# First MLP's weights, split a whole slice at a time, with one buffer place per slice

## The chip, the cores and the metric

The kernel runs on one core of one Trainium2 chip. The metric is the device time of one launch in microseconds (us); lower is better. Three runs of the kernel before took 896.28, 899.64 and 904.32 us, and their median, 899.64 us, is the time before.

## The reference

Windowed attention (4 batches, 8 heads, 576 positions, head dimension 64; the first four heads see the last 32 positions, the last four every fourth of the last 128), then two MLPs, 512 to 2048 to 512, over all 2304 tokens, in float32:

```python
attn = softmax(where(masks, q @ k.T / sqrt(64), -1e9))
x = concat_heads(attn @ v)                 # 2304 x 512
h = maximum(x @ w_in, 0.0)
x = (h * h) @ w_out                        # first MLP
h = x @ w_in2
out = (h * cos(h)) @ w_out2                # second MLP
```

## The kernel before

Attention is cut into 48 units (4 batches, 4 head pairs, 3 groups of 192 queries). A unit goes through eight steps (`unit`, L184): S matmuls (L198, and for the first twelve units a mask matmul, L205), row maximum on VectorE (DVE, L219, L221), three Exp on ScalarE (ACT, L225), reciprocal and product on DVE (L230 to L237), a transpose on TensorE (PE, L242), a copy on ACT (L245), the value matmuls (L254), and the split of the result into two float32r parts, `xh` by a cast on ACT (L281) and `xl` by a subtraction on DVE (L283).

The 2304 tokens are five blocks of 512, 384, 512, 512 and 384 columns (`SIZES`), the hidden layer 16 slices of 128 (`fc`). One step of a block is one slice: `product1` (L305) makes a slice of h with 12 matmuls (4 chunks of 128 rows, times wh·xh, wh·xl, wl·xh), `middle` (L317) applies the activation and splits the result into `gh` (ACT, L351) and `gl` (DVE, L353), `product2` (L359) adds the slice to y with 12 more. The first twelve units are all of the first block's tokens, so its `product1` has to wait for them; the other 36 are worked in between the steps of the first four blocks.

Weights come as 64-bit words. `load_w` (L99) loads one half of a slice (i = 0 is w_in, i = 1 is w_out; 512 KB) with one DMA on SyncE's queue (SP). `split_w` (L108) turns it into the parts wh and wl in four steps: two DVE instructions that build a float32 (L116, L119), a third (L122), a cast on ACT (L125) and a subtraction on DVE (L127), each on 512 columns. The words lie in a pool of three buffers (`raw`, shared with `store` and `load_x`), but the first six halves (`RAW_EARLY`) and the first twelve units (`N_EARLY`) lie in places of weights of later slices (`early`, L91). The parts of one half have one tile, `w{fc}_{i}`; the second MLP's weights go into the same tiles when the last block of the first MLP is through with them.

The order of the work is written by hand. `at` puts a call on a list with a time in steps (16 steps to a block; t = 0 is the first block's start), and `in_steps` does so for a generator's parts. `before` turns a number on a finer scale into a time before t = 0. The list is sorted and run. Up to t = 0 and from t = 96 each engine's instructions stand in just that order; between these, for the first MLP and the first block of the second, the framework's scheduler may move an instruction ahead of one that its own model holds up (L505 to L509). Every engine and the SP queue work in order. The weights' times are:

```python
EARLY_LOADS = (2.5, 3.5, 6.62, 8.91, 10.16, 11.56)
EARLY_SPLITS = (5.5, 7, 17.91, 21.32, 23.16, 24.98)
t = h / 2 - 1.573                        # later halves, h = 2 * fc + i
times = [t + d for d in SPLIT]           # SPLIT = (0, 0.05, 0.2, 0.62)
at(split_at[h - 3] + 0.01 ..., load_w, *w)
```

An entry of `EARLY_LOADS` is a place among the units' loads, which are numbered 1 to 11: 3.5 is between units 3 and 4.

Of the kernel before, what the change touches and what calls it, by code (L numbers as in the profile page):

```python
# [7 lines left out]
F32 = mybir.dt.float32  # L8
F32R = mybir.dt.float32r
BF16 = mybir.dt.bfloat16  # L10
U32 = mybir.dt.uint32
# [5 lines left out]
P = 128  # L17
B, H, S, D = 4, 8, 576, 64
DM, DFF = 512, 2048
# [4 lines left out]
KT = 96  # L24
# [3 lines left out]
UQ = TPU * QT  # L28
UK = QT * (TPU - 1) + KT
UP = TPU * 2 * QT  # L30
UV = TPU * 2 * D
# [5 lines left out]
NF = DFF // P  # L37
# [3 lines left out]
SLOT = [0, 2, 1, 0, 2]  # L41
PACE = [n / max(SIZES) for n in SIZES]
N_EARLY = 12
RAW_EARLY = 6
SQUARE_ON_ACT = (0, 4)
LAG = (2, 3)
EPS = 1e-9
# [9 lines left out]
def attention_moe_moe(ctx: ExitStack, tc: tile.TileContext, units, masks, ident16_in, ident_in, w1, w2, out):  # L57
    nc = tc.nc
    pool = lambda name, bufs, **k: ctx.enter_context(tc.tile_pool(name=name, bufs=bufs, **k))
    const = pool("const", 1)  # L60
    wpool = pool("weights", 1)
    raw = pool("raw", 3)
    wtmp = pool("wtmp", 2)
# [16 lines left out]
    def at(t, f, *a):  # L80
        events.append((t, len(events), f, a))
# [6 lines left out]
    magic = const.tile([P, 1], F32, name="magic")  # L88
    y1 = [dram.tile([P, NC, n], F32, name=f"y1_{k}") for k, n in enumerate(SIZES)]

    def early(i):  # L91

        return dict(tag=f"w{NF - 1 - i // 2}_{1 - i % 2}", name="early")


    weights = {}
    raws = {}

    def load_w(m, fc, i):  # L99
        if m == 0 and 2 * fc + i < RAW_EARLY:  # L100
            t = wpool.tile([P, DM, 2], U32, **early(N_EARLY * 3 // 2 + 2 * fc + i))
        else:
            t = raw.tile([P, DM, 2], U32, tag="raw", name="wraw")
        raws[m, fc, i] = t
        nc.sync.dma_start(
            out=t, in_=(w1, w2)[m][fc, i].bitcast(U32).rearrange("p (n t) -> p n t", t=2))

    def split_w(m, fc, i):  # L108


        words = raws.pop((m, fc, i))
        low, high = words[:, :, 0], words[:, :, 1]
        parts = wpool.tile([P, 2, DM], F32R, tag=f"w{fc}_{i}", name=f"w{fc}_{i}")
        hi, lo = weights[m, fc, i] = parts[:, 0, :], parts[:, 1, :]
        t = wtmp.tile([P, DM], U32, tag="t", name="wt")
        nc.vector.tensor_scalar(  # L116
            out=t, in0=high, scalar1=3, scalar2=0x3FFFFFF8,
            op0=ALU.logical_shift_left, op1=ALU.bitwise_and)
        nc.vector.scalar_tensor_tensor(  # L119
            out=t, in0=high, scalar=0xC0000000, in1=t, op0=ALU.bitwise_and, op1=ALU.bitwise_or)  # L120
        yield
        nc.vector.scalar_tensor_tensor(  # L122
            out=t, in0=low, scalar=29, in1=t, op0=ALU.logical_shift_right, op1=ALU.bitwise_or)
        yield
        nc.scalar.copy(out=hi, in_=f32(t))  # L125
        yield
        nc.vector.tensor_tensor(out=lo, in0=f32(t), in1=f32(hi), op=ALU.subtract)  # L127
        yield


    xs = {}

    def block(m, k):
        if (m, k) not in xs:
            s = SLOT[k]
            xs[m, k] = tuple(
                ring.tile([P, NC, SIZES[k]], F32R, tag=f"x{n}{s}", name=f"x{n}{s}") for n in "hl"
            )
        return xs[m, k]
# [4 lines left out]
    def load_unit(u):  # L144
        if u >= N_EARLY:
            t = upool.tile([P, UQ + UK], F32, tag="uq", name="uq")
            nc.sync.dma_start(out=t, in_=units[u // UNITS, u % UNITS, :, :UQ + UK])
            loaded[u] = t, None
            return

        t = wpool.tile([P, UQ + UK], F32, **early(u // 2 * 3 + u % 2))
        nc.sync.dma_start(out=t, in_=units[0, u, :, :UQ + UK])
        if u == 0:
            nc.sync.dma_start(out=ident16, in_=ident16_in)
            nc.sync.dma_start(out=mask[:, :4 * KT], in_=masks[:, :4 * KT])
        loaded[u] = t
        if u % 2:
            v = wpool.tile([KT, 2, UV], F32, **early(u // 2 * 3 + 2))
            nc.sync.dma_start(
                out=v, in_=units[0, u - 1:u + 1, :KT, UQ + UK:].rearrange("u p n -> p u n"))  # L160
            for i in range(2):
                loaded[u - 1 + i] = loaded[u - 1 + i], v[:, i, :]
        if u == 1:
            nc.sync.dma_start(out=ident, in_=ident_in)
            nc.sync.dma_start(out=mask[:, 4 * KT:], in_=masks[:, 4 * KT:])
# [6 lines left out]
    def bank():  # L172
        return ps_h.tile([P, 512], F32, tag="h", name="h")

    def y_bank(e):
        return ps_y.tile([P, 512], F32, tag=f"y{e}", name=f"y{e}")
# [118 lines left out]
    def in_steps(times, key, steps, *a):  # L295
        for i, t in enumerate(times):
            at(t, *((resume, key) if i else (start, key, steps, *a)))
# [6 lines left out]

    def product1(m, k, fc):  # L305
        xh, xl = block(m, k)
        wh, wl = weights[m, fc, 0]
        h = hs[m, k, fc] = bank()[:, :SIZES[k]]
        for c in range(NC):
            for i, (w, x) in enumerate(((wh, xh), (wh, xl), (wl, xh))):  # L310
                nc.tensor.matmul(  # L311
                    h, w[:, c * P:(c + 1) * P], x[:, c, :],
                    start=c == 0 and i == 0, stop=c == NC - 1 and i == 2)
            if c:
                yield
# [42 lines left out]

    def product2(m, k, fc):  # L359
        gh, gl = gs.pop((m, k, fc))  # L360
        wh, wl = weights[m, fc, 1]
        if fc == 0:
            ys[m, k] = [y_bank(e)[:, :SIZES[k]] for e in range(NC)]
        y = ys[m, k]
        for e in range(NC):
            n = 0
            for w, g in ((wh, gh), (wh, gl), (wl, gh)):
                nc.tensor.matmul(  # L368
                    y[e], w[:, e * P:(e + 1) * P], g,
                    start=fc == 0 and n == 0, stop=fc == NF - 1 and n == 2,  # L370
                )
                n += 1
# [37 lines left out]
    before = lambda x: (x - 26.284) / 4.7  # L410

    load_unit(0)
    constants()
    for u in range(1, N_EARLY):
        at(before(-3.5 + 0.01 * u), load_unit, u)
# [14 lines left out]
    def later_by(t, d):  # L430

        while d:
            k = int(t // NF) if d > 0 else -int(-t // NF) - 1
            pace = PACE[k % NB]
            edge = (k + 1) * NF - t if d > 0 else k * NF - t
            move = d / pace
            if abs(move) <= abs(edge):
                return t + move
            t += edge
            d -= edge * pace  # L440
        return t
    for u in range(UNITS * B):
        if u < N_EARLY:
            t = 1.3 * u if u < 2 else 3.877 + 1.656 * (u - 2)
            times = [before(t + d) for d in (0, 1, 2.07, 2.87, 4.24, 4.95, 5.32, 6.2)]
        else:
            i = later.index(u)
            t, t1, t2 = place[i:i + 3]
            times = [t, *(later_by(t, d) for d in (0.25, 0.75, 0.8)),
                     t1 + 0.003, later_by(t1, 0.15), t2 - 0.003, later_by(t2, 0.42)]  # L450
            at(later_by(t, -1.5), load_unit, u)
            at(later_by(t, 0.6), load_values, u)
        in_steps(times, u, unit, u)


    EARLY_LOADS = (2.5, 3.5, 6.62, 8.91, 10.16, 11.56)
    EARLY_SPLITS = (5.5, 7, 17.91, 21.32, 23.16, 24.98)
    SPLIT = (0, 0.05, 0.2, 0.62)
    split_at = []
    for h in range(2 * NF):  # L460
        w = (0, h // 2, h % 2)
        if h < RAW_EARLY:
            at(before(-3.5 + 0.01 * EARLY_LOADS[h]), load_w, *w)
            times = [before(EARLY_SPLITS[h] + d) for d in (0, 0.6, 1.35, 2.24)]
        else:
            t = h / 2 - 1.573
            times = [t + d for d in SPLIT]
            at(split_at[h - 3] + 0.01 if h >= RAW_EARLY + 3 else before(-1. + 0.01 * h), load_w, *w)
        split_at.append(times[0])
        in_steps(times, ("w", *w), split_w, *w)  # L470
    t1 = NB * NF

    N_FAST = 12
    split_at = sorted(
        (t1 - NF + 1.2 + 1.3 * fc + 0.7 * max(fc - N_FAST, 0) + 1.8 * i, (1, fc, i))
        for fc in range(NF) for i in range(2)
    )
    for h, (t, w) in enumerate(split_at):
        in_steps([t + d for d in SPLIT], ("w", *w), split_w, *w)
        at(t - 1.5, load_w, *w)  # L480
    for m in range(2):
        for k in range(NB):
            t = (m * NB + k) * NF
            for fc in range(NF):
                times = [t + fc] * (NC - 1)
# [96 lines left out]
```

## Time and profile before

| | us |
|---|---|
| median of three runs | 899.64 |
| the profiled execution, whole | 898.14 |
| its span (first to last instruction) | 895.2 |
| PE busy | 880.6 |
| DVE busy | 527.5 |
| ACT busy | 456.8 |

The time outside the span of the profiled execution is 2.94 us. Busy times are sums over the span, in which the start (attention of the first block), the first MLP (with the remaining units) and the second MLP follow each other. Ends of matmuls are modelled in this profile, so the distance between the starts of matmuls says more than the busy share. TensorE's granted clock is full (1.0) throughout.

### The profile page before, as it was taken

What the parts mean: (1) busy time and instruction counts of PE and PEld (TensorE: products, weight loads), DVE (VectorE), ACT (ScalarE), POOL (GpSimd) and SP (SyncE); (2) the same over time, 40 slices, a digit from 0 to 9 for tenths busy, and PEclk for the clock granted to TensorE, in tenths of its full rate; (3) what the DMA queues carried; (4) which work ended last, traced back from release to release, by engine and by line L of the source; (5) the groups of instructions that cost most, each with busy time, mean ns of one, the idle gap of its engine ahead of it and who ended that gap; (6) DMA issues with size and microseconds to landing.
All of it is one profiled execution on the core that took longest, in us unless ns stands there. A gap on an engine that the chain in (4) does not pass through costs nothing.

```text
span 895.2 us, 13547 instructions
## 1 busy us (share of the span) xinstructions
PE 880.6 (98%) x5161; PEld 762.0 (85%) x5161; DVE 527.5 (59%) x1082; ACT 456.8 (51%) x1101; POOL 47.7 (5%) x84
## 2 busy tenths in 40 slices
PE   7899999999999999999999999999999999999998
PEld 4578888999888888888999888899988888888998
DVE  6999974454434434222799995455554555555554
ACT  5687775544433432222555664455555555445554
POOL 0000000000000000000000111111111111111110
PEclk9999999999999999999999999999999999999999
DMA  9766632211211112000576520020020002000100
GB/s 261 231 184 211 210 100 81 65 49 49 85 34 33 40 31 94 1 1 1 178 219 203 163 83 1 1 94 1 2 82 1 1 1 82 1 1 1 48 1 36
DMA packets 27680, 66.27 MB, mean 74 GB/s; under 512 B 3168, under 2 KB 15328, under 8 KB 27616
## 3 DMA queue, kind: packets, MB, share of 16 engines
q1 hardware_dynamic: 27616, 65.42, 24.0%
q8 instruction: 40, 0.66, 0.3%
q14 instruction: 24, 0.20, 0.1%
HBM read 55.97 MB, written 9.44 MB: 73 GB/s over the span
## 4 chain that ended last, share of the span: by engine, by line
PE 89%; DVE 4%; DMA 4%; ACT 1%; issue 1%; SPq 0%; ACTq 0%
PE y L368 42%; PE h L311 41%; PE h L198 3%; DMA early<-units 3%; PE h L254 2%; PE h L242 2%; DVE wt L119 1%; DVE w L127 1%; DVE wt L122 1%; DVE wt L116 1%; DMA wraw<-w 1%; DMA xraw<-y 0%; DVE gl L353 0%; ACT w L125 0%; ACT r L323 0%
## 5 line engine op out<-in xcount | busy, mean ns | idle before, releaser
L368 PE MATMUL y<-gh,w 128*128 128x512 f32 (+1 forms) x1280 | 395.1, 370 | 2.7 <-ACT gh L351 2.6
L311 PE MATMUL h<-xh,w 128*128 128x512 f32 (+1 forms) x1280 | 395.6, 370 | 0.4 <-ACT xh L281 0.4
L368 PEld LDWEIGHTS y<-gh,w 128*128 128x128 f32 x1280 | 237.5, 188 | 33.8 <-ACT gh L351 3.6
L311 PEld LDWEIGHTS h<-xh,w 128*128 128x128 f32 x1280 | 237.5, 188 | 30.7 <-ACT xh L281 0.6
L368 PE MATMUL y<-gl,w 128*128 128x512 f32 (+1 forms) x640 | 235.4, 368 | 0.2 <-DVE gl L353 0.2
L311 PE MATMUL h<-xl,w 128*128 128x512 f32 (+1 forms) x640 | 235.6, 368 | 0.0
L342 DVE TENSOR_TENSOR r<-h,r 128x512 f32<-128x512 f32 (+1 forms) x128 | 82.0, 641 | 168.4 <-ACT r L339 94.6
L353 DVE TENSOR_TENSOR gl<-r,gh 128x512 fp32r<-128x512 f32 (+1 forms) x160 | 102.6, 641 | 125.3 <-ACT gh L351 124.1
L351 ACT CAST gh<-r 128x512 fp32r<-128x512 f32 (+1 forms) x160 | 92.2, 576 | 92.2 <-PE y L368 79.3
L311 PEld LDWEIGHTS h<-xl,w 128*128 128x128 f32 x640 | 120.2, 188 | 15.4 <-DVE xl L283 0.4
L368 PEld LDWEIGHTS y<-gl,w 128*128 128x128 f32 x640 | 120.2, 188 | 15.2 <-DVE gl L353 0.5
L338 ACT ACTIVATE r<-r 128x512 f32<-128x512 f32 (+1 forms) x80 | 47.2, 590 | 147.0 <-DVE r L335 147.0
L323 ACT ACTIVATE r<-h 128x512 f32<-128x512 f32 (+1 forms) x80 | 44.2, 554 | 103.2 <-PE h L311 102.9
L330 POOL TENSOR_SCALAR kf<-kf 128x512 f32<-128x512 f32 (+1 forms) x80 | 47.5, 594 | 836.8 <-ACT kf L329 831.8
L329 ACT ACTIVATE kf<-h,magic 128x512 f32<-128x512 f32 (+1 forms) x80 | 51.0, 638 | 19.3 <-PE h L311 19.1
L339 ACT ACTIVATE r<-r,halfpi 128x512 f32<-128x512 f32 (+1 forms) x80 | 54.3, 680 | 2.4
L333 DVE SCALAR_TENSOR_TENSOR r<-kf,h 128x512 f32<-128x512 f32 (+1 forms) x80 | 50.0, 626 | 4.7 <-POOL kf L330 4.7
L335 DVE SCALAR_TENSOR_TENSOR r<-kf,r 128x512 f32<-128x512 f32 (+1 forms) x80 | 50.9, 638 | 2.5
L125 ACT CAST w<-wt 128x512 fp32r<-128x512 f32 x64 | 39.4, 618 | 23.8 <-DVE wt L122 23.7
L127 DVE TENSOR_TENSOR w<-wt,w 128x512 fp32r<-128x512 f32 x64 | 43.6, 685 | 4.8 <-ACT w L125 4.4
L225 ACT ACTIVATE p<-p,nm 128x96 f32<-128x96 f32 x108 | 39.4, 366 | 12.1 <-DVE nm L219 11.1
L122 DVE SCALAR_TENSOR_TENSOR wt<-wraw,wt 128x512 uint32<-128x512 uint32 x58 | 40.6, 700 | 0.4
(49 smaller groups left out, 502.4 us busy)
## 6 DMA issues: line engine op xcount, KB each, us to landing
wraw<-w SPq DMA_DIRECT2D x58, 512.0 KB, 4.2
uq<-units SPq DMA_DIRECT2D x36, 208.0 KB, 2.9
uv<-units SPq DMA_DIRECT2D x36, 144.0 KB, 2.2
early<-w SPq DMA_DIRECT2D x6, 512.0 KB, 8.9
y<-o SPq DMA_DIRECT2D x6, 512.0 KB, 2.7
xraw<-y SPq DMA_DIRECT2D x6, 512.0 KB, 5.0
out<-o SPq DMA_DIRECT2D x6, 512.0 KB, 2.8
early<-units SPq DMA_DIRECT2D x12, 208.0 KB, 8.2
```

Of the source, the lines that this page charges most:

```text
L122: nc.vector.scalar_tensor_tensor(out=t, in0=low, scalar=29, in1=t, op0=ALU.logical_shift_right, op1=ALU.bitwise_or)
L127: nc.vector.tensor_tensor(out=lo, in0=f32(t), in1=f32(hi), op=ALU.subtract)
L311: nc.tensor.matmul(h, w[:, c * P:(c + 1) * P], x[:, c, :], start=c == 0 and i == 0, stop=c == NC - 1 and i == 2)
L329: nc.scalar.activation(out=kf, in_=h, func=AF.Identity, bias=magic, scale=INV2PI)
L330: nc.gpsimd.tensor_scalar(out=kf, in0=kf, scalar1=-MAGIC, scalar2=1.0, op0=ALU.add, op1=ALU.mult)
L333: nc.vector.scalar_tensor_tensor(out=r, in0=kf, scalar=-C1, in1=h, op0=ALU.mult, op1=ALU.add)
L335: nc.vector.scalar_tensor_tensor(out=r, in0=kf, scalar=-C2, in1=r, op0=ALU.mult, op1=ALU.add)
L339: nc.scalar.activation(out=r, in_=r, func=AF.Sin, bias=halfpi, scale=-1.0)
L342: nc.vector.tensor_tensor(out=r, in0=h, in1=r, op=ALU.mult)
L351: nc.scalar.copy(out=gh, in_=r)
L353: nc.vector.tensor_tensor(out=gl, in0=r, in1=f32(gh), op=ALU.subtract)
L368: nc.tensor.matmul(y[e], w[:, e * P:(e + 1) * P], g, start=fc == 0 and n == 0, stop=fc == NF - 1 and n == 2,)
```

## The change

In the first MLP slices 0 to 13 are loaded and split whole. `load_both` puts both halves' words (two DMAs, as before) into the place of a later slice, given by `RAW_AT`; `split_both` does the same four steps on both halves in one instruction each (1024 columns), and its scratch tile lies in the place of the next slice. Slices 14 and 15, and all of the second MLP's, go half by half as before. The parts of a slice have one tile, `w{fc}`, in place of two. The first twelve units lie pairwise in such places. The loads are issued 2.2 steps ahead of the split, or when the place's last words are split; the order of the early loads and the times of the splits change, and those of the second MLP's splits.

```diff
-RAW_EARLY = 6
+RAW_EARLY = 3
+RAW_AT = [9, 8, 7, 6, 15, 14, 13, 12, 15, 14, 13, 15, 14, 15]
...
+    def place_of(fc, shape, dtype, name):
+        return wpool.tile(shape, dtype, tag=f"w{fc}", name=name)
...
+    def load_both(fc):
+        t = raws[fc] = place_of(RAW_AT[fc], [P, 2, DM, 2], U32, "words")
+        for i in range(2):
+            nc.sync.dma_start(out=t[:, i], in_=words_of(0, fc, i))
...
+    def parts_of(m, fc):
+        if (m, fc) not in weights:
+            weights[m, fc] = place_of(fc, [P, 2, 2, DM], F32R, f"w{fc}")
+        return weights[m, fc]
...
+    def split_both(fc):
+        words = raws.pop(fc)
+        t = place_of(fc + 1, [P, 2, DM], U32, "wt")
+        parts = parts_of(0, fc)
+        yield from decode(
+            words[:, :, :, 0], words[:, :, :, 1], t, parts[:, :, 0, :], parts[:, :, 1, :])
...
+        n = UQ + UK
+        if u % 2 == 0:
+            raws["u"] = place_of(NF - 1 - u // 2, [P, 4 * DM], F32, "early")
+        pair = raws["u"]
+        t = pair[:, u % 2 * n:(u % 2 + 1) * n]
...
+            v = pair[:KT, 2 * n:2 * n + 2 * UV].rearrange("p (u n) -> p u n", u=2)
...
-    EARLY_LOADS = (2.5, 3.5, 6.62, 8.91, 10.16, 11.56)
-    EARLY_SPLITS = (5.5, 7, 17.91, 21.32, 23.16, 24.98)
+    EARLY_LOADS = (2.5, 7.5, 11.5)
+    EARLY_SPLITS = (6.2, 19, 23.4)
+    EARLY_STEPS = (0, 1.2, 1.9, 3.2)
+    STEPS = (0, 0.2, 0.3, 0.85)
...
+    for fc in range(len(RAW_AT)):
+        if fc < RAW_EARLY:
+            t = before(-3.5 + 0.01 * EARLY_LOADS[fc])
+            times = [before(EARLY_SPLITS[fc] + d) for d in EARLY_STEPS]
         else:
+            times = [fc - 1.7 + d for d in STEPS]
+            t = before(-1) if fc == RAW_EARLY else times[0] - 2.2
+            if RAW_AT[fc] in RAW_AT[:fc]:
+                last = max(i for i in range(fc) if RAW_AT[i] == RAW_AT[fc])
+                t = max(t, split_at[last] + 0.25)
...
+        at(t, load_both, fc)
+        in_steps(times, ("w", fc), split_both, fc)
+    for h in range(2 * len(RAW_AT), 2 * NF):
+        t = h / 2 - 1.573
+        at(t - 2.2, load_w, 0, h // 2, h % 2)
...
-    N_FAST = 12
+    N_FAST = 10
...
-        (t1 - NF + 1.2 + 1.3 * fc + 0.7 * max(fc - N_FAST, 0) + 1.8 * i, (1, fc, i))
+        (t1 - NF + 2.6 + 1.3 * fc + 0.7 * max(fc - N_FAST, 0) + 0.65 * i, (1, fc, i))
```

`decode` is the body of the old `split_w` (L116 to L127); `product1` and `product2` take their parts from the slice's one tile.

## Rows read from the trace of the kernel before

**Rows 1.** The page, part 1: busy us (share of span) and instructions of each engine.
```profile
PE 880.6 (98%) x5161; PEld 762.0 (85%) x5161; DVE 527.5 (59%) x1082; ACT 456.8 (51%) x1101; POOL 47.7 (5%) x84
```
**Rows 2.** Busy time by stretch: us, each engine (instructions), clock, DMA share, GB/s.
```profile
10.00:20.00 10.00, 7.15 (x111) 5.39 (x109) 9.55 (x29) 7.52 (x33) 0.00 (x0) 1.00 1.07 282
...
40.00:50.00 10.00, 6.98 (x46) 5.05 (x43) 9.81 (x25) 8.24 (x27) 0.00 (x0) 1.00 0.31 91
...
100.00:110.00 10.00, 10.00 (x65) 8.11 (x64) 9.78 (x23) 7.14 (x22) 0.00 (x0) 1.00 0.69 214
```
**Rows 3.** PE's waits from 0 to 50 us: total us, times, longest.
```profile
PE h L198 <- DMA early<-units: 3.9, 6, 1.2
PE y L368 <- ACT gh L351: 2.6, 1, 2.6
...
PE h L311 <- ACT xh L281: 0.4, 1, 0.4
```
**Rows 4.** The chain that ended last, one stretch: start us, us, what.
```profile
59.21 2.72 PE h L311 x12
61.93 0.50 PE h L254 x12
62.43 0.70 PE h L198 x12
63.13 0.46 PE h L242 x3
```
**Rows 5.** Groups by line and shape, 0 to 240 us: busy us, mean ns | idle before.
```profile
L353 DVE TENSOR_TENSOR gl<-r,gh 128x512 fp32r<-128x512 f32 x17 | 11.7, 691 | 9.0 <-ACT gh L351 8.5
L353 DVE TENSOR_TENSOR gl<-r,gh 128x384 fp32r<-128x384 f32 x16 | 8.9, 556 | 12.8 <-ACT gh L351 12.8
L116 DVE TENSOR_SCALAR wt<-wraw 128x512 uint32<-128x512 uint32 x26 | 10.9, 420 | 0.1
L119 DVE SCALAR_TENSOR_TENSOR wt<-wraw,wt 128x512 uint32<-128x512 uint32 x26 | 17.8, 683 | 0.1
L127 DVE TENSOR_TENSOR w<-wt,w 128x512 fp32r<-128x512 f32 x32 | 21.8, 684 | 0.7 <-ACT w L125 0.2
L125 ACT CAST w<-wt 128x512 fp32r<-128x512 f32 x32 | 19.7, 616 | 7.1 <-DVE wt L122 7.0
```
**Rows 6.** DVE's instructions in order of time, five of them: start us, us, what.
```profile
10.77 0.42 DVE L116 TENSOR_SCALAR wt<-early 128x512 uint32<-128x512 uint32 x1
...
18.64 0.45 DVE L219 TENSOR_REDUCE nm<-h 128x3 f32<-128x288 f32 x1
...
26.02 0.46 DVE L219 TENSOR_REDUCE nm<-h 128x3 f32<-128x288 f32 x1 [0.57 <-PE h L205]
...
31.43 0.45 DVE L219 TENSOR_REDUCE nm<-h 128x3 f32<-128x288 f32 x1
...
56.80 0.68 DVE L127 TENSOR_TENSOR w<-wt,w 128x512 fp32r<-128x512 f32 x1
```
**Rows 7.** PE's instructions in order of time, four of them.
```profile
24.98 0.77 PE L198 MATMUL h<-early 64*64 64x96 f32 x12 [0.54 <-DMA early<-units]
...
30.24 0.49 PE L311 MATMUL h<-xh,w 128*128 128x512 f32 x1
...
36.29 0.51 PE L242 MATMUL h<-ident,p 128*96 128x128 f32 x3 [0.59 <-DVE p L237]
...
45.87 1.19 PE L368 MATMUL y<-gh,w 128*128 128x512 f32 x4 [2.61 <-ACT gh L351]
```
**Rows 8.** ACT's instructions in order of time, two of them.
```profile
40.76 0.57 ACT L281 CAST xh<-y 128x32 fp32r<-128x32 f32 x4
...
43.80 0.62 ACT L125 CAST w<-wt 128x512 fp32r<-128x512 f32 x1
```
**Rows 9.** Busy time by stretch, the second MLP's first block.
```profile
520.00:530.00 10.00, 10.00 (x46) 8.29 (x45) 9.93 (x18) 6.55 (x13) 1.24 (x2) 1.00 0.40 105
```
**Rows 10.** PE's one wait from 450 to 650 us.
```profile
PE y L368 <- DVE gl L353: 0.2, 1, 0.2
```

More of the change, by code (lines that the diff above doesn't have):

```diff
@@ L89, in attention_moe_moe, with words_of, decode @@
     y1 = [dram.tile([P, NC, n], F32, name=f"y1_{k}") for k, n in enumerate(SIZES)]
-    def early(i):
-        return dict(tag=f"w{NF - 1 - i // 2}_{1 - i % 2}", name="early")
+    def place_of(fc, shape, dtype, name):
+        return wpool.tile(shape, dtype, tag=f"w{fc}", name=name)
     weights = {}
     raws = {}
+    def words_of(m, fc, i):
+        return (w1, w2)[m][fc, i].bitcast(U32).rearrange("p (n t) -> p n t", t=2)
     def load_w(m, fc, i):
[L100 to L115, printed above, removed]
+        t = raws[m, fc, i] = raw.tile([P, DM, 2], U32, tag="raw", name="wraw")
+        nc.sync.dma_start(out=t, in_=words_of(m, fc, i))
+    def load_both(fc):
+        t = raws[fc] = place_of(RAW_AT[fc], [P, 2, DM, 2], U32, "words")
+        for i in range(2):
+            nc.sync.dma_start(out=t[:, i], in_=words_of(0, fc, i))
+    def decode(low, high, t, hi, lo):
         nc.vector.tensor_scalar(
@@ L128, in split_w @@
         yield
+    def parts_of(m, fc):
+        if (m, fc) not in weights:
+            weights[m, fc] = place_of(fc, [P, 2, 2, DM], F32R, f"w{fc}")
+        return weights[m, fc]
+    def split_w(m, fc, i):
+        words = raws.pop((m, fc, i))
+        t = wtmp.tile([P, DM], U32, tag="t", name="wt")
+        parts = parts_of(m, fc)[:, i]
+        yield from decode(words[:, :, 0], words[:, :, 1], t, parts[:, 0, :], parts[:, 1, :])
+    def split_both(fc):
[4 more added lines that the diff above has]
+            words[:, :, :, 0], words[:, :, :, 1], t, parts[:, :, 0, :], parts[:, :, 1, :])
     xs = {}
@@ L149, in load_unit @@
             return
-        t = wpool.tile([P, UQ + UK], F32, **early(u // 2 * 3 + u % 2))
-        nc.sync.dma_start(out=t, in_=units[0, u, :, :UQ + UK])
+        n = UQ + UK
[3 more added lines that the diff above has]
+        t = pair[:, u % 2 * n:(u % 2 + 1) * n]
+        nc.sync.dma_start(out=t, in_=units[0, u, :, :n])
         if u == 0:
@@ L157, in load_unit @@
         if u % 2:
-            v = wpool.tile([KT, 2, UV], F32, **early(u // 2 * 3 + 2))
+            v = pair[:KT, 2 * n:2 * n + 2 * UV].rearrange("p (u n) -> p u n", u=2)
             nc.sync.dma_start(
-                out=v, in_=units[0, u - 1:u + 1, :KT, UQ + UK:].rearrange("u p n -> p u n"))
+                out=v, in_=units[0, u - 1:u + 1, :KT, n:].rearrange("u p n -> p u n"))
             for i in range(2):
@@ L306, in product1 @@
         xh, xl = block(m, k)
-        wh, wl = weights[m, fc, 0]
+        wh, wl = (weights[m, fc][:, 0, n, :] for n in range(2))
         h = hs[m, k, fc] = bank()[:, :SIZES[k]]
@@ L360, in product2 @@
         gh, gl = gs.pop((m, k, fc))
-        wh, wl = weights[m, fc, 1]
+        wh, wl = (weights[m, fc][:, 1, n, :] for n in range(2))
         if fc == 0:
@@ L453, in attention_moe_moe @@
         in_steps(times, u, unit, u)
-    EARLY_LOADS = (2.5, 3.5, 6.62, 8.91, 10.16, 11.56)
-    EARLY_SPLITS = (5.5, 7, 17.91, 21.32, 23.16, 24.98)
+    EARLY_LOADS = (2.5, 7.5, 11.5)
+    EARLY_SPLITS = (6.2, 19, 23.4)
+    EARLY_STEPS = (0, 1.2, 1.9, 3.2)
+    STEPS = (0, 0.2, 0.3, 0.85)
     SPLIT = (0, 0.05, 0.2, 0.62)
     split_at = []
[L460 to L464, printed above, removed]
-        else:
-            t = h / 2 - 1.573
-            times = [t + d for d in SPLIT]
-            at(split_at[h - 3] + 0.01 if h >= RAW_EARLY + 3 else before(-1. + 0.01 * h), load_w, *w)
-        split_at.append(times[0])
-        in_steps(times, ("w", *w), split_w, *w)
+    for fc in range(len(RAW_AT)):
+        if fc < RAW_EARLY:
+            t = before(-3.5 + 0.01 * EARLY_LOADS[fc])
+            times = [before(EARLY_SPLITS[fc] + d) for d in EARLY_STEPS]
+        else:
+            times = [fc - 1.7 + d for d in STEPS]
[3 more added lines that the diff above has]
+                t = max(t, split_at[last] + 0.25)
+        split_at.append(times[0])
+        at(t, load_both, fc)
[3 more added lines that the diff above has]
+        at(t - 2.2, load_w, 0, h // 2, h % 2)
+        in_steps([t + d for d in SPLIT], ("w", 0, h), split_w, 0, h // 2, h % 2)
     t1 = NB * NF
-    N_FAST = 12
+    N_FAST = 10
     split_at = sorted(
-        (t1 - NF + 1.2 + 1.3 * fc + 0.7 * max(fc - N_FAST, 0) + 1.8 * i, (1, fc, i))
+        (t1 - NF + 2.6 + 1.3 * fc + 0.7 * max(fc - N_FAST, 0) + 0.65 * i, (1, fc, i))
         for fc in range(NF) for i in range(2)
```

## The prediction

> **What bounds the kernel now.** I read the page first: PE is busy for 880.6 of 895.2 us of the span, DVE for 527.5 [rows 1]. A busy share proves little where ends are modelled, so next comes the chain that ended last. From 46 us on its pieces are runs of twelve matmuls that start 2.72 us apart, 0.227 us a matmul, with the parts of one attention unit between them (0.50 + 0.70 + 0.46 us), and nothing else for most of the way [rows 4]: a step of two runs and a unit takes 7.1 us. PE's waits then say where it stands still. From 0 to 50 us there are six kinds, 3.9 us for the units' loads, 2.6 us for the first gh, down to 0.4, together 10.6 us [rows 3]. From 50 us to 450 the list of waits is empty, and from 450 to 650 it holds one of 0.2 us [rows 10]. So all that can be won without fewer matmuls lies before 45.87 us, when the first `product2` begins [rows 7].
>
> What holds that point back? In the busy times by stretch DVE has 9.55 us of 10 between 10 and 20 us and 9.81 between 40 and 50, while PE has some 7 [rows 2]. DVE is full in the start, and its queue is in order. It is also full from 50 to 120 us (9.78 of 10), but there PE loses nothing by it.
>
> **The change, part by part.**
>
> *Wider splits.* Nothing in this trace is 1024 columns wide, so I take the growth from gl, 0.556 us for 384 columns and 0.691 for 512: 1.055 ns a column, and 0.54 us for 512 more [rows 5]. L119, L122 and L127 then go from 0.69 to 1.23 us. L116 (0.42) lies between 0.42 and 0.84 for two halves; I take 0.69, half of the others' growth, as its 512 columns cost 0.42 where the others' cost 0.68. A slice is 2 x (0.42 + 3 x 0.69) = 4.98 us on DVE before and 0.69 + 3 x 1.23 = 4.38 after, 0.6 us less; fourteen slices give 8.4 us. The ends are 0 (twice the width, twice the time) and 2.49 us a slice (the width is free). ACT's cast (0.616) lies between 0.62 and 1.23; with DVE's growth it is 1.16, and almost nothing is saved. Of the fourteen, slices 3 to 13 run behind a full PE: 0. If that cover were gone, they would be worth 11 x 0.6 = 6.6 us. Slices 0 to 2 lie in the start: at most 1.8 us off the path there.
>
> *Order of the early loads.* Bytes and the number of DMAs stay. A half of 512 KB takes 2.1 us at some 250 GB/s (282 in one stretch [rows 2]). Counting the halves ahead of each unit in the list: unit 3 gets one more (2.1 us later), unit 7 one less, unit 8 one more, unit 11 one less; the rest stay. Unit 11 comes 2.1 us sooner, but at that point DVE is behind, not the load. Unit 8 landed before about 24.98 - 2.1 - 0.85 = 22.0 us (unit 9's S began at 24.98 on its landing [rows 7]; one half and 208 KB lie between) and lands at 24.1 now.
>
> *The start on DVE, in its order.* I walk the list and mark four places.
> (a) Row maximum of unit 5, at 18.64 us before [rows 6]. Before, the first half's L116 began at 10.77, so its words were there [rows 6], and its three instructions filled a gap. Now the split needs both halves: the second lands at about 12.8. From there stand in the queue (small instructions by the distance of their starts in DVE's order of time) L116 and L119 (1.9), unit 3's maximum (0.6), unit 2's product (0.9), L122 (1.2), a small xl (0.3), unit 4's maximum (0.6), unit 3's product (0.9) and L127 (1.2): 20.4, which is 1.8 us later, although the sum of the work fell.
> (b) Maximum of unit 9, at 26.02, after 0.57 us of waiting: four units in 6.8 us, 1.7 each [rows 6]. Unit 8's is due at 20.4 + 5.1 = 25.5; its load permits 24.1 + 1.04 (from S to maximum for unit 9, rows 6 and 7) = 25.1. Unit 9 follows at 27.2, 1.2 us late.
> (c) Maximum of unit 11, at 31.43, 5.4 us further [rows 6]. Three instructions of a half (1.8 us) leave this stretch and two of a whole slice (1.9) enter: 32.7, 1.3 us late.
> (d) Transpose of unit 11, at 36.29 [rows 7]. From (c) come 2.2 us of attention and L122 (1.2): DVE is at 36.1. A wait is added here: ACT's cast for slice 1 stands in ACT's queue ahead of unit 9's xh and unit 10's copy, and waits for that L122. Behind it are the cast (1.16), xh (0.5), the copy (0.5) and unit 10's value matmuls (0.5), and PE's transpose of unit 11 is behind those: 38.8, 2.5 us late.
> (e) xh of unit 11, at 40.76 [rows 8]. Transpose, nine matmuls of `product1` (9 x 0.227 = 2.0) and value matmuls give 3.1: 41.9, 1.1 us late. The time is won back because slice 2's cast now stands behind this xh and not ahead of it.
> (f) First `product2`, at 45.87 [rows 7], 5.1 us after (e). A cast of 0.62 us between the two in ACT's queue goes [rows 8]: 41.9 + 5.1 - 0.6 = 46.4. DVE's xl of unit 11 may be later than its xh, since L116, L119 and L122 of slice 2 (3.2 us) stand ahead of it; that end is +1.4.
> I take +0.6 us for the start. Its ends: -1.8 (only the saved work counts) and +1.4.
>
> *Whole slices before `product1`.* It now waits for both halves. Before, the tightest second half, slice 4's, ended at 57.48 [rows 6], and `product1` of slice 4 began at 59.21 [rows 4]: 1.7 us of lead even for the half that it did not need. In the list a whole slice ends 0.85 step before its use, a second half before 0.453: 0.4 step or 2.8 us sooner. Cost 0; if the lead went, PE would wait by what is missing.
>
> *Loads into places.* Slices 8 to 13 wait on SP for the L122 of a slice three, four or two before. Behind such a load stand the units' loads. The list leaves at least 1.75 steps, 12.4 us, for two DMAs, some 4.2 us by the time of a half above. Cost 0, up to 3 us once if DVE lags a step. POOL has no work in this stretch (x0) [rows 2].
>
> *Second MLP.* Its first split moves from 1.2 to 2.6 steps after the last block's start, at most 1.4 x 5.4 = 7.6 us, and its cast waits until `product2` has left the place, which the list allows for by a tenth of a step. DVE is full there (9.93 of 10 [rows 9]). Slice 15 is ready by the list about four steps before its use. PE's wait of 0.2 us [rows 10] may go, or grow by one half's four instructions, 2.5 us; I take 0.
>
> Sum: 898.14 (span 895.2 and 2.94 around it) + 0.6 = 898.7. The median of the three runs is 1.5 us above that execution. I name 899.0.
>
> **Rivals.**
> 1. *DVE's saving is felt in the start.* If the order costs nothing, 1.8 us go, and with unit 11 early about half of the 3.9 us of waits for loads [rows 3]: -3.8, 894.3. For it: DVE is full there. Against it: the split now waits for two halves.
> 2. *DVE paces the first MLP after all.* Then slices 3 to 13 give 6.6 us: 892.1. PE's weight loads are busy for 8.11 us of 10 between 100 and 110 us [rows 2], which leaves room; but runs start 2.72 us apart without a wait [rows 4]. The Trainium skill (Perfetto Trace Analysis, Identifying the Most-Contended Engine) has matmul busy time as a poor measure of what PE has left and wants the share of weight loads read instead; by that rule PE has a fifth to spare and this rival holds, while the trace's empty list of waits speaks against it.
> 3. *Slower: wide instructions in front of the first gl.* After t = 0 the scheduler may put L119 and L122 of slice 3 ahead of gl of slice 0, and its cast ahead of gh. Each is twice as wide now: 2 x 1.23 + 1.16 = 3.6 us more, +4.2 with the start's 0.6: 902.3. It decides if both stand before L353's first on DVE and that L353 comes after 48 us.
> 4. *The paired units don't load freely.* If reading one unit held up the loading of its neighbour in the same place, six pairs would each lose some 2 us: +12, 910.7 with the start. Against it: `product1` reads the first chunks of xh at 30.24 [rows 7], while ACT still writes that tile at 40.76 [rows 8]; so parts of a tile are told apart.
>
> **How the numbers follow.** Forecast (start within -1.8 and +1.4, rest unmoved) 0.59, rival 1 0.18, rival 2 0.05, rival 3 0.13, rival 4 0.05. A measurement of this kernel tells about 1%, 9 us, from no change. Over 1% faster needs nearly all of PE's 10.6 us of waiting, or rival 2 with 1: 0.04. Over 1% slower is rival 4 and a little of rival 3: 0.06. The range takes in rivals 1 and 3 and the runs' own spread of some 4 us either way: 894 to 904.
>
> **What would show it.** After: L119 on 1024 columns at 1.2 us, 72 splits' instructions on DVE in the first MLP for 128; unit 3's S later, unit 11's load no longer awaited; the first `product2` within 44.1 to 47.3 us; runs of twelve matmuls 2.72 us apart after it and no PE wait up to 450 us; DVE below 9.2 of 10 between 100 and 110 us with PE unmoved. I am wrong if the first `product2` moves by more than 2 us, if PE waits for L127 anywhere, or if runs come closer together.

## The result

The changed kernel takes 905.95 us (median of ten runs, 903.79 to 910.3), the kernel before 898.52 in the same session: a ratio of 1.0085 [1.0066, 1.0104]. The forecast was 899.0, with 894 to 904 as its range. It is wrong: the kernel became slower, by more than the 4.2 us of rival 3 and in another way. The execution profiled after took 905.74 us, so 7.6 more than the one of [rows 1].

First the page, part 1, and the groups of the wide instructions over the whole span.

```profile
PE 886.4 (98%) x5161; PEld 765.2 (85%) x5161; DVE 520.9 (58%) x1026; ACT 455.4 (50%) x1087; POOL 49.1 (5%) x84
```
```profile
L127 DVE TENSOR_TENSOR w<-wt,w 128x1024 fp32r<-128x1024 f32 x14 | 17.1, 1220 | 2.5 <-ACT w L125 2.3
L122 DVE SCALAR_TENSOR_TENSOR wt<-words,wt 128x1024 uint32<-128x1024 uint32 x14 | 17.0, 1217 | 0.0
L119 DVE SCALAR_TENSOR_TENSOR wt<-words,wt 128x1024 uint32<-128x1024 uint32 x14 | 17.0, 1220 | 0.1
L125 ACT CAST w<-wt 128x1024 fp32r<-128x1024 f32 x14 | 14.7, 1048 | 4.5 <-DVE wt L122 4.4
L116 DVE TENSOR_SCALAR wt<-words 128x1024 uint32<-128x1024 uint32 x14 | 9.6, 685 | 0.0
```

DVE lost 6.6 us of work against [rows 1], and its four wide instructions have the durations that were estimated. But PE is busy 5.8 us longer for the same 5161 matmuls. Since nothing was added to PE, this points to a PE that ran slower somewhere. Here are PE's waits from 0 to 60 us (the answer to [rows 3]) and the busy times by stretch; after the five engines, the first number is the granted clock.

```profile
PE y L276 <- ACT pts L267: 5.2, 5, 2.3
PE h L264 <- ACT p L256: 1.9, 1, 1.9
PE h L264 <- DVE p L259: 1.6, 2, 1.4
```
```profile
32.00:36.00 4.00, 2.01 (x30) 1.19 (x28) 3.97 (x9) 1.95 (x11) 0.00 (x0) 1.00 1.04 370
36.00:40.00 4.00, 1.69 (x14) 1.19 (x16) 4.00 (x11) 1.76 (x5) 0.00 (x0) 0.65 1.03 348
40.00:44.00 4.00, 4.00 (x34) 2.99 (x30) 3.40 (x10) 1.01 (x4) 0.00 (x0) 0.50 0.73 266
44.00:48.00 4.00, 3.87 (x29) 2.68 (x30) 3.17 (x8) 1.67 (x11) 0.00 (x0) 1.00 0.86 252
48.00:52.00 4.00, 2.12 (x8) 1.27 (x7) 3.59 (x7) 4.00 (x9) 0.00 (x0) 0.86 1.00 326
52.00:56.00 4.00, 4.00 (x15) 3.15 (x14) 3.73 (x5) 2.53 (x5) 0.00 (x0) 0.72 0.62 202
```

Two things stand there that [rows 2] and [rows 3] did not have. PE waits 2.3 us for unit 10's copy (pts). And the granted clock, 1.00 in every stretch of the start before, falls in the stretch of that wait (0.65), is at its lower level (0.50, 1.2 of 2.4 GHz) from 40 to 44 us, behind it, and falls again behind the wait that ends at 50.65 us. PE's instructions in order of time show both.

```profile
39.56 0.91 PE L276 MATMUL y<-pts,early 96*64 96x64 f32 x12 [2.27 <-ACT pts L267]
40.40 0.88 PE L264 MATMUL h<-ident,p 128*96 128x128 f32 x3
...
45.71 0.57 PE L276 MATMUL y<-pts,early 96*64 96x64 f32 x12
...
50.65 0.31 PE L264 MATMUL h<-ident,p 128*96 128x128 f32 x1 [1.88 <-ACT p L256]
...
55.37 0.40 PE L390 MATMUL y<-gh,w 128*128 128x512 f32 x1
```

The three transposes of unit 11 at 40.40 take 0.88 us; at full clock they took 0.51 [rows 7]. Who is late? DVE's instructions in order of time, from the maximum of unit 11 on:

```profile
33.01 0.45 DVE L241 TENSOR_REDUCE nm<-h 128x3 f32<-128x288 f32 x1
...
33.66 0.69 DVE L116 TENSOR_SCALAR wt<-words 128x1024 uint32<-128x1024 uint32 x1
34.27 0.17 DVE L253 RECIPROCAL rs<-rs 128x3 f32<-128x3 f32 x1
34.39 1.23 DVE L119 SCALAR_TENSOR_TENSOR wt<-words,wt 128x1024 uint32<-128x1024 uint32 x1
35.53 0.45 DVE L259 TENSOR_TENSOR p<-p,rs 128x288 f32<-128x288 f32 x1
...
36.49 1.23 DVE L122 SCALAR_TENSOR_TENSOR wt<-words,wt 128x1024 uint32<-128x1024 uint32 x1
37.62 0.17 DVE L252 TENSOR_SCALAR rs<-sm 128x3 f32<-128x3 f32 x1
37.69 1.22 DVE L122 SCALAR_TENSOR_TENSOR wt<-words,wt 128x1024 uint32<-128x1024 uint32 x1
38.83 0.17 DVE L253 RECIPROCAL rs<-rs 128x3 f32<-128x3 f32 x1
38.91 0.67 DVE L116 TENSOR_SCALAR wt<-words 128x1024 uint32<-128x1024 uint32 x1
39.49 0.46 DVE L259 TENSOR_TENSOR p<-p,rs 128x288 f32<-128x288 f32 x1
```

L116 and L119 at 33.66 and 34.39 and the L122 at 37.69 belong to slice 3, the L116 at 38.91 to slice 4. By the text they come after t = 0, so behind all that is shown. The part up to t = 0 is written out by hand, and front and forecast took its order as fixed; but what the scheduler places freely afterwards it also places between those instructions, if what it needs is there (e1 and e4 below test this). Slice 3's words (place 6) and scratch (place 4) are free from the beginning, while before, each half's scratch had to wait for one of two buffers. So 3.8 us of DVE's work (0.69 + 1.23 + 1.22 + 0.67) moved ahead of the products p of units 10 and 11, and the L122 at 36.49, slice 1's, is late. ACT's cast waits for that one, with unit 9's xh and unit 10's copy in its queue behind it:

```profile
37.74 1.04 ACT L125 CAST w<-wt 128x1024 fp32r<-128x1024 f32 x1 [2.77 <-DVE wt L122]
38.70 0.49 ACT L303 CAST xh<-y 128x128 fp32r<-128x128 f32 x3
39.01 0.50 ACT L267 COPY pts<-h 96x384 f32<-96x384 f32 x1
```

At the first MLP's last block (its first matmul on 384 columns) the kernel after is 6.28 us behind the one before (429.63 against 423.35 us). Between 60 us and there PE waits nowhere. It then waits 1.4 us for the first gh of the second MLP, and ends 7.6 us later.

### The profile page after: what moved, and what is told of

It reads as the page before. It is cut to its first block, busy times and chain, and to the rows that moved or that the text cites. A ratio compares the mean times of both kernels' runs of the same rounds, so it can differ in the third digit from the quotient of the medians.

```text
span 903.6 us, 13466 instructions
## 1 busy us (share of the span) xinstructions
PE 886.4 (98%) x5161; PEld 765.2 (85%) x5161; DVE 520.9 (58%) x1026; ACT 455.4 (50%) x1087; POOL 49.1 (5%) x84
## 4 chain that ended last, share of the span: by engine, by line
PE 90%; DVE 5%; DMA 2%; ACT 2%; issue 1%; SPq 0%; DVEq 0%; ACTq 0%
PE y L390 41%; PE h L333 40%; PE h L220 3%; PE h L264 2%; PE h L276 2%; DMA wraw<-w 1%; DVE wt L122 1%; DVE wt L119 1%; DVE wt L116 1%; DVE w L127 1%; DMA xraw<-y 1%; DMA early<-units 0%; DVE gl L375 0%; PE y L276 0%; DVE nm L241 0%
## 5 line engine op out<-in xcount | busy, mean ns | idle before, releaser
L125 ACT CAST w<-wt 128x512 fp32r<-128x512 f32 (+1 forms) x50 | 37.0, 740 | 23.9 <-DVE wt L122 22.6
L127 DVE TENSOR_TENSOR w<-wt,w 128x512 fp32r<-128x512 f32 (+1 forms) x50 | 41.7, 840 | 4.8 <-ACT w L125 4.5
L267 ACT COPY pts<-h 96x384 f32<-96x384 f32 x48 | 22.8, 475 | 18.3 <-PE h L264 17.4
```

## The experiments

All medians stand beside the kernel before on the same chip. The last three columns are of one execution each, the profiled one: its time, which can lie off the median; "start", its delay at the first matmul of the last block of the first MLP, against 423.35 us in the profiled execution before (898.14 us, granted clock 1.00 throughout); and "T 11", the start of unit 11's transpose (36.29 before).

```
kernel                        median   ratio [95%]             profiled  start   T 11
after                         905.95   1.0085 [1.0066, 1.0104]  905.74    6.28   40.40
e1  scratch late              906.37   1.0063 [1.0035, 1.0091]  905.52    7.83   40.12
e2  second MLP's times back   907.98   1.0086 [1.0052, 1.0120]  905.73    5.58   41.69
e3  nine idle matmuls         906.25   1.0090 [1.0056, 1.0124]  905.43    7.74   43.36
e4  before, scratch free      905.17   1.0055 [1.0035, 1.0074]  902.30    5.48   38.85
e5  slices 0-2 by halves      903.58   1.0044 [1.0021, 1.0067]  901.88    3.51   37.48
e6  e1 + cast behind unit 10  900.98   1.0012 [0.9993, 1.0030]  902.23    3.54   39.84
e7  places alone              900.51   1.0015 [0.9996, 1.0033]  898.97    1.18   36.16
e8  e1 + loads by half        907.62   1.0092 [1.0063, 1.0121]  908.16    8.72   41.67
e9  cast behind unit 10       904.87   1.0071 [1.0053, 1.0089]  903.48    5.45   42.45
e10 e6 + slice 0 by halves    900.33   1.0024 [1.0002, 1.0046]  904.33    3.67   39.94
e11 e6 + second MLP later     901.47   1.0025 [1.0008, 1.0042]  903.41    4.67   40.97
e12 before, wait filled       897.98   0.9987 [0.9968, 1.0005]  897.62    0.23   37.07
e13 e7, wait filled           899.66   1.0000 [0.9986, 1.0013]  897.06   -0.04   36.86
e14 before, wait filled by 8  897.58   0.9985 [0.9968, 1.0001]  897.46   -0.35   36.53
e15 after, wait filled by 5   902.88   1.0029 [1.0011, 1.0047]  903.45    5.10   40.73
e16 e1, both waits filled     901.52   1.0011 [0.9990, 1.0031]  901.57    1.57   38.74
```

**The hoisted split, e1 and e4.** e1 moves slice 3's scratch to a place that comes free only when slice 2's words have been read (and slice 4's to another); e4 does the opposite to the kernel before, where slice 3's halves get a scratch of their own that is free from the start.

```diff
-        t = place_of(fc + 1, [P, 2, DM], U32, "wt")
+        t = place_of({3: 7, 4: 6}.get(fc, fc + 1), [P, 2, DM], U32, "wt")
```
```diff
+        if m == 0 and fc == 3:
+            t = wpool.tile([P, DM], U32, tag=f"w15_{i}", name="wt")
```

> The changed kernel, with the scratch tiles of slices 3 and 4 in the places where the words of slices 2 and 3 lie, so that their splits cannot begin before those are done. Theory A (the splits of slices 3 and 4, whose words and scratch are free from the start, are moved by the scheduler into the chain of units 10 and 11, and the start is late by their work and what follows from it): those instructions stand behind unit 11's xl on VectorE, TensorE's waits before 50 us fall from 12.2 to 6 to 8 us, the first product2 comes some 5 to 6 us earlier, and the time falls from 905.9 to 899 to 901 us. Theory B (a whole slice in one instruction is itself what costs: the wait for both halves and the long instructions): 904 to 907 us, as before the edit.

> The kernel before, with the scratch tiles of slice 3's two halves in a place that is free from 10 us on; nothing else is changed. Theory A: the scheduler now moves slice 3's splits ahead of the products of units 10 and 11, some 4 us of VectorE work in the chain that holds the first product2 back; that comes 3 to 6 us later and the time is 901.5 to 905 us. Theory B (the order of these few instructions does not matter): 897.5 to 899.5 us, no change.

In e4 slice 3's halves do stand between units 10 and 11, PE waits 2.5 us for p of unit 11, and the kernel before becomes 5 us slower: the hoist alone can do it.

```profile
38.85 0.50 PE L245 MATMUL h<-ident,p 128*96 128x128 f32 x3 [2.51 <-DVE p L240]
```

But e1 is no faster than the kernel after, though the hoist is gone from DVE's order. Its time lies in theory B's band; theory B's reason, the whole splits themselves, falls with e6 below, which keeps them. A second cause must be enough by itself.

**Slice 1's cast, e6 and e9.** Both begin slice 1's split 1.2 units of the time axis sooner and put its cast behind unit 10's copy; e6 has e1's scratch as well, e9 hasn't.

```diff
             times = [before(EARLY_SPLITS[fc] + d) for d in EARLY_STEPS]
+            if fc == 1:
+                times = [before(x) for x in (17.8, 18.9, 22.12, 23.05)]
```

> The kernel after with slice 3's scratch late, and slice 1's split begun 1.2 units of the time axis sooner with its ScalarE cast behind unit 10's copy instead of ahead of unit 9's. Theory A (TensorE's 2.2 us wait ahead of unit 10's PV, and the half clock behind it, come from that cast): the wait for pts falls under 1 us, the clock stays above 0.9 from 36 to 44 us, and the time is 902 to 904.5 us. Theory B (VectorE's doubled chain is late whatever ScalarE does): 905 to 907.5 us.

> The kernel after with slice 1's split begun sooner and its cast behind unit 10's copy, and nothing else: slice 3's scratch is free from the start again, so its whole split stands between the attention's instructions of units 10 and 11. Theory A (two separate causes, each enough: the hoist delays p of unit 10 and 11 whatever ScalarE does): T of unit 11 at 41 to 43 us, TensorE's wait for p over 2 us, 903 to 906 us. Theory B (the cast alone was the cause, the hoist hides): 900 to 902 us, as with the scratch late.

With both causes gone the time is 901.0 us, below both bands; with one of them left it stays at 904.9 (hoist) or 906.4 (cast). In e9 PE's wait only changes its place:

```profile
PE h L264 <- DVE p L259: 3.5, 1, 3.5
```

So the two are alternatives, not terms of a sum: each makes PE stand for over 2 us between 35 and 40 us. e6's median is back within 0.12% of the kernel before, but this doesn't show that a late chain is free: its profiled execution has unit 11 3.5 us late, the start 3.54 us late, and ends 4.1 us late.

What comes behind a late chain is another matter. In the profiles of after, e1 to e5, e7, e8 and e15 the clock falls below 1.00 somewhere between 44 and 60 us, and between T 11 and the start their delay grows by 0.2 to 4.0 us. In those of e6, e9 to e14 and e16 it is 1.00 all through these 16 us, and the delay changes by -0.9 to 0.0 us.

**The clock, e3, e12 and e13 to e16.** Idle matmuls, whose product is thrown away when the next matmul starts in the same accumulator, fill PE's waits and are meant to add nothing to a chain (the kernel before has thirteen of them, L182, in its first 9 us). e3 puts nine ahead of unit 10's value matmuls in the kernel after, e15 five; e16 puts five there and seven ahead of the first `product2` in e1; e12 and e14 put nine and eight ahead of the first `product2` in the kernel before, e13 eight in e7.

```diff
         if not first:
             v = loaded.pop(u)
+        if u == 10:
+            for _ in range(5):
+                nc.tensor.matmul(pv, idle[:, :P], idle, start=True, stop=True)
```
```diff
         y = ys[m, k]
+        if m == 0 and k == 0 and fc == 0:
+            seen = block(0, 0)[1][:, 3, :].bitcast(BF16)[:, :512]
+            for _ in range(7):
+                nc.tensor.matmul(y[0], idle[:, :P], seen, start=True, stop=True)
```

> The changed kernel with nine idle 512-column matmuls in front of unit 10's value matmuls, where TensorE stands still for 2.3 us before its clock falls to half. Theory A (part of the loss is TensorE's clock: at 1.2 GHz the transpose of unit 11, two matmuls of product1 and 18 S matmuls take 1.5 us longer, all on the chain): the granted clock between 36 and 44 us is 0.9 to 1.0 instead of 0.58, the first product2 comes 1.5 to 2 us earlier and the time is 903.5 to 904.5 us. Theory B (VectorE and ScalarE set the end, so the clock costs nothing): the clock rises as well, and the time stays at 905.5 to 906.5 us.

> The kernel after with five idle matmuls in TensorE's 2.3 us wait ahead of unit 10's PV (1.15 us at full clock, 2.1 at half). Theory A (the half clock behind the wait is part of the loss: from T of unit 11 to PV of unit 11 the kernel after took 5.3 us, the variant without the late cast, at full clock, 3.95): the clock is full from 40 to 46 us, PV of unit 11 1.0 to 1.4 us sooner, 904.4 to 905.2 us. Theory B (the late chains alone, the clock costs nothing): 905.5 to 907 us though the clock is full.

> The variant with slice 3's scratch late (906.37 us) with five idle matmuls ahead of unit 10's PV and seven ahead of the first product2. Theory A: the clock is full from 40 to 56 us, the first product2s take 2.9 us instead of 5.4, and the time falls by the two, 2.5 to 3.9 us, to 902.5 to 904 us. Theory B: 905.5 to 907 us though the clock is full.

e3 misled. Its nine matmuls began at half clock (the three ahead of them stand 0.43 us apart), took 3.30 us in a wait of 2.27, and made unit 10 later themselves. With five, the kernel after falls to a ratio of 1.0029, and e1 with both waits filled falls from 1.0063 to 1.0011. Both times lie below the bands of theory A. The gain is some 5 us each by the ratios, 3.1 and 4.9 us by the medians. Not all of it is the clock behind the filled wait. Of the 2.3 us between the profiled executions of after and e15, 1.2 are won at the start and 1.0 in the second MLP's wait for its first gh (0.4 for 1.4 us), which no idle matmul touches; e16's start is 6.3 us sooner than e1's, of which 1.4 lie ahead of unit 11's transpose.

First PE in e1, then in e16, at the first `product2`, and e16's clock (1.00) in that stretch:

```profile
51.36 1.72 PE L390 MATMUL y<-gh,w 128*128 128x512 f32 x4 [2.26 <-ACT gh L373]
52.88 0.63 PE L390 MATMUL y<-gl,w 128*128 128x512 f32 x1
53.31 0.63 PE L390 MATMUL y<-gh,w 128*128 128x512 f32 x1
...
55.34 0.39 PE L390 MATMUL y<-gl,w 128*128 128x512 f32 x1
```
```profile
45.43 1.68 PE L393 MATMUL y<-xl,idle 128*128 128x512 bf16 x7
47.13 1.20 PE L397 MATMUL y<-gh,w 128*128 128x512 f32 x4
48.17 0.39 PE L397 MATMUL y<-gl,w 128*128 128x512 f32 x1
48.40 0.39 PE L397 MATMUL y<-gh,w 128*128 128x512 f32 x1
...
49.53 0.39 PE L397 MATMUL y<-gl,w 128*128 128x512 f32 x1
```
```profile
44.00:48.00 4.00, 3.98 (x21) 2.32 (x22) 3.27 (x6) 3.12 (x7) 0.00 (x0) 1.00 0.99 330
```

The first eleven matmuls start within 3.98 us in the one and 2.40 in the other: behind the wait they stood 0.43 us apart, at half clock, and 0.23 behind the idle ones. (The 5.4 us of e16's expectation are sixteen matmuls, its 2.9 us twelve.) e16's start is 1.57 us late, e1's 7.83.

The Trainium skill (TensorE: Matmul & The Clock Gate, HAM oscillation — how this bites in real kernels) describes such a thing, with longer waits than here: groups of matmuls that each start at the lower clock because each comes behind a wait for data, with half of the throttled time as the price. The trace agrees: 1.58 us of those 3.98 were lost, nearly half, as the last of the eleven were back at full clock.

Executions without a trace speak of the clock too, since each has its mean granted clock on record. Of 104 executions of the kernel before, in five sessions, the eight at 1.000 have a median of 897.05 us and the twelve at 0.988 to 0.990 one of 903.38; a straight line through all of them falls by 0.53 us for each 0.001. The ten of the kernel after stand at 0.984 to 0.994. On average they are 6.7 us above the kernel before, and 3.8 us above its line at their own clock. By this estimate, which is a correlation and not an experiment, some 3 us go with the clock and some 4 with the later chain; e1 and e9 are 3.9 and 3.2 us above the line, e6 1.1.

> The kernel before with nine idle matmuls in TensorE's 2.6 us wait ahead of the first product2, which add no work to the chain. Theory A (in part of the executions the clock falls to half behind that wait, as in the profile of the variant with single places, where the first product2s took 1.3 us longer): the clock is full from 44 to 50 us, and the median is 0.5 to 1.3 us below the kernel before. Theory B (that wait does not set the clock, or the clock there costs nothing): within 0.4 us.

> The kernel before with eight idle matmuls in the same wait (nine ended 0.05 us after the wait could have ended). Theory A (in part of the executions the clock falls behind that wait): 897.6 to 898.8 us and a ratio to the kernel before of 0.998 to 0.9993, with fewer executions above 902 us. Theory B (the wait does not set the clock there): a ratio of 0.9997 to 1.0005.

The kernel before has such a wait too, 2.6 us [rows 3]. In its profiled execution the clock stayed at 1.00 behind it; in e7's, with the same wait and the same work, it fell to 0.65 from 44 to 48 us.

```profile
44.00:48.00 4.00, 2.27 (x5) 1.82 (x6) 3.81 (x10) 3.97 (x13) 0.00 (x0) 0.65 0.01 1
```

Filled, the median is 0.13% and 0.15% lower; both intervals just include 1, so the gain is likely and not shown. One of e14's twelve executions is above 902 us, as is one of 23 of the kernel before beside it, so fewer late executions are not shown either. These two, at 898.0 and 897.6, are the lowest medians of all.

**The places, e7 and e13.** e7 is the kernel before with one place per slice and the units in pairs, all splits by halves.

> The kernel before with one place per slice and the paired units, every split half by half: no whole split, no words in places beyond slice 2. Theory A (one place per slice costs only the second MLP's first product2 its wait of 1.3 us): the start as before, first product2 at 45.5 to 46.5 us, the wait for gh at 505 to 510 us there, 899 to 901.5 us against 898.5 to 900 of the kernel before. Theory B (places cost nothing anywhere, the second MLP's wait comes from elsewhere): ratio within 0.1% of 1. Theory C (units tracked as pairs cost the start): 903 us or more.

> The variant with single places alone (900.5 us) with eight idle matmuls in TensorE's wait ahead of the first product2. Theory A (the places cost only the second MLP's wait of some 0.9 us; what the start lost in that profile, 1.2 us, was the clock): the clock is full from 44 to 50 us, the start as before to 0.4 us, 898.6 to 899.8 us, some 0.9 above the kernel before with the same fill. Theory B (places cost the start too): 900 us or more, and the start 1 us behind though the clock is full.

With the wait filled, e13's start is as early as before, and its ratio to the unfilled kernel before is 1.0000. But like with like is e14, the kernel before with the same fill in the same session: 897.58 against 899.66 us, 2.1 us where theory A had 0.9. The executions overlap (896.5 to 904.0, 897.06 to 901.7), so single places and paired units cost some 2 us or nothing; this stays open. The 12 us of rival 4 they don't cost. The second MLP's wait for its first gh is 0.9 us in e7, 0.3 in e13, 0.9 in e14 (halves) and 2.4 in e16, so it isn't the places' alone; what sets its length stays open. Putting back the second MLP's old split times (e2: 907.98 us, wait 1.3) or moving its splits of slices 11 to 15 behind its first steps on ACT (e11: 901.47, e6 with a wait of 0.8 instead of 1.6) gave nothing that shows.

**The early splits and loads, e5, e8, e10.** e5 splits and loads slices 0 to 2 by halves at the old times, with e1's scratch; e10 does that for slice 0 in e6; e8 gives e1 the old order of the loads alone.

> The kernel after with slices 0 to 2 loaded and split half by half at the old times again, and with slice 3's scratch in a place that comes free late; slices 3 to 13 stay whole, each slice has one place. Theory A (all of the start's loss lies in the whole splits, casts and loads of slices 0 to 2 and in the hoisted split of slice 3): T of unit 11 at 36 to 37 us, first product2 at 46 to 47.5 us (slice 3's whole split still stands ahead of the first gl, some 0.8 us), no half clock before 50 us, and with the second MLP's 1.3 us the time is 899 to 902 us. Theory B (the whole splits from slice 3 on, or the single places, cost the time): 904 to 907 us.

> The variant of 901.0 us (scratch late, cast behind unit 10) with slice 0 loaded and split half by half at the old times; all other slices whole. Theory A (what is left of the start's loss is slice 0's whole split, which waits for both halves' words and holds VectorE ahead of units 3 and 4): T of unit 11 at 37 to 38 us instead of 39.8, no wait of TensorE for unit loads over 1 us, 898.5 to 900 us. Theory B (the rest lies behind T of unit 11): 900.5 to 902 us.

> The kernel after with slice 3's scratch late, and the words of slices 0 to 2 loaded as two halves at the old places in the queue; splits whole. Theory A (the second half of slice 0 ahead of unit 3 and of later units starves the attention's start): TensorE's waits for unit loads at 12 to 16 us fall from 3.3 us to under 1 and the time is 903 to 905 us. Theory B (loads are early enough either way): 905.5 to 907.5 us, with the same waits.

e8's waits for the units' loads fell to 0.6 us in all (3.3 in e1), as its theory A had it, but the time didn't fall: these waits were not what held the start back. e10's 900.33 lies between its bands and within e6's runs, and its T 11 is where e6's is. e5 hit neither band. Its first `product2` comes 9.57 us after T 11, against 9.58 before, so slice 3's L116 and L119, which stand ahead of the first gl there, cost nothing. 1.6 us of its 3.5 are half clock: the first twelve matmuls of `product2` start within 4.22 us (47.05 to 51.27), where they took 2.64 before.

## Why the prediction was wrong

**What held.** The instructions cost what was estimated (1.22 for 1.23, 0.685 for 0.69, the cast 1.05 for 1.16). Steps (a) to (c) came at 20.59, 27.34 and 33.01 us for 20.4, 27.2 and 32.7. From 60 us up to the second MLP PE waits nowhere, so the whole slices ahead of `product1` and the loads into places cost 0, as said. Slices 3 to 13 gave DVE time (9.31 us of 10 between 100 and 110 us, for "below 9.2") that PE had no use for: its runs of twelve still start 2.72 us apart. So rival 2 fell. The rule of the Trainium skill (Perfetto Trace Analysis, Identifying the Most-Contended Engine) that spoke for it, by which the share of weight loads shows what PE has left, is not borne out here: weight loads are busy 85% of the span after as before, though DVE has less to do. Rival 4 fell with e7, 900.5 us for 910.7.

**The step that failed is (d), and with it (e) and (f).** (d) had unit 11's transpose at 38.8 us, from the order of the text and with PE at full clock. It came at 40.40, xh of unit 11 at 46.33 for 41.9, and the first `product2` at 55.37 for 46.4 (4.7 us of it slice 2's `product1`, which now stands ahead, and would take 2.7 at full clock). Two things were missing:
- The scheduler doesn't keep to the line at t = 0. Rival 3 came nearest: its sign, slice 3's L119 and L122 ahead of a first gl later than 48 us, is met (51.57 us), and its price was 902.3 us. But it had the wide split in the way behind t = 0 and just ahead of the first gl. It stands ahead of units 10 and 11, where it holds up the last of the attention, and at the place that rival 3 named L116 and L119 cost nothing (e5).
- A wait of PE was priced by its length alone. That the cast would hold up unit 10 was in (d), as 2.5 us. What came behind the wait, matmuls at 1.2 GHz, was in no term; by the mean clocks some 3 us go with it.

e16 is the test of the rest: without the hoisted split and with the clock at 1.00 from 36 to 56 us, the maxima of units 5, 9 and 11 come at 20.02, 27.58 and 33.24 us, unit 11's transpose at 38.74 for 38.8, the first `product2` at 47.13 for 46.4, and the start is 1.57 us late, against 0.6 with an end of +1.4. The walk through DVE's queue comes out within 0.8 us for the kernel that the text describes. The kernel that was built had another order, and PE another clock. The hoist is worth 3.9 us by medians and 5.3 by ratios (e9 to e6) once the cast is out of the way, and nothing that shows while it is there (e1); the fills are worth 3 to 5 us (after to e15, e1 to e16), and the clock some 3 by the mean clocks. The shares overlap, as both go through the same waits, and don't add up to the 7.4 us of the medians.

The reasoning for a small effect, that only the first 46 us can be won, was also one for a large loss: where PE has short waits, one more of 2 us can change the speed of what follows.

## To carry to other kernels

Give every instruction in a freely scheduled part something that it must wait for, or expect it as early as its inputs and its buffer allow; a change that frees a buffer moves work, and the built order has to be read before queues are walked. Price a new wait of PE with what it does to the clock behind it, and look at the granted clock by stretches of a few us before saying that a chain is late. Where such a wait can't go, matmuls that lead nowhere may fill it, if they are shorter than the wait at half clock.

## What the runs showed of the hardware

The granted clock fell behind waits of PE of some 2 us in the start, but not behind each: in the profiled execution before it stayed at 1.00 behind 2.6 us, and the same wait in e7 was followed by matmuls 0.43 us apart. One program's mean clock differs between executions: the kernel before's runs from 0.988 to 1.00, and its time with it. With idle matmuls in the wait the clock stayed at 1.00 there in all of e12, e13, e14 and e16. Between 12 and 24 us it fell in many variants, to 0.59 from 12 to 16 us and 0.56 from 16 to 20 in e13, whose start is as early as before: there PE is not what sets the pace. Idle matmuls run at whatever clock is granted: nine of them took 3.30 us in e3, where they began at half clock, and 2.12 in e12.
